# The assumed delay of an instruction page in an issue-order planner: SLOW from 7000 to 8900, FAST from 3500 to 3900

## The chip, the cores and the metric

One core of a Trainium2 chip runs the whole program. The metric is the time of one execution in device microseconds, as the median of several runs. Five engines work side by side and meet at semaphores: TensorE (PE for its matmuls, PEld for its weight loads), VectorE (DVE), ScalarE (ACT), GpSimd (POOL) and SyncE (SP), which here only issues DMAs.

## What is computed

A decaying linear attention over 2 batches, 8 heads, 768 positions and 64 values a head, in blocks with a running state, and behind it two small networks on the 1536 tokens of 512 values, all in fp32:

```python
intra = einsum(einsum(q_b, k_b) * Dmask, v_b);  inter = einsum(q_b * lam_pow, kv_state)
out_b = intra + inter                                 # attention, block by block
kv_state = lam_block * kv_state + einsum(k_b * rev_pow, v_b)
x = (sigmoid(x @ w_gate) * (x @ w_val)) @ w_out       # 512 -> 1536 -> 512
h = x @ w_in2;  y = where(h > 0, h, exp(min(h, 0)) - 1) @ w_out2   # 512 -> 2048 -> 512
```

## The kernel before

**Work.** The attention goes through six chunks of 128 positions (`for c in range(NCH)`). For a chunk, `scores` multiplies keys and queries (tile `st`) and, from the second chunk on, the decayed keys `kd` with the values of the chunk before (written to the same banks, so also `st` in a profile); VectorE applies the decay (`pr`), TensorE multiplies by the values and by the state (tile `x`; the state is `sn`), and `split_chunk` makes the operands of the first network from the result. These attention products are plain fp32: each takes two passes, and so four instructions (two weight loads, two matmuls), on few columns. A block of 16 or 32 of them is issued in one piece (`together`).

The networks run on fp32r operands split into a high and a low part, three products for one, with a seven-product scheme for 2x2 blocks (`product`) and with `unit` for the output matrices. The first group of gate and value weights is multiplied without that scheme for the first two chunks (`direct`): 24 matmuls of 256 columns for each of gate and value and each chunk, two instructions each. In the profile they carry the tile names `direct` and `warm`, since the bank A0 was first named by the 18 warm-up matmuls that open the kernel.

**Order.** Nothing runs as it is recorded. The program's engine calls only record operations (`Work.record`, hence one line, L182, stands for nearly all instructions in the profile). `Work.issue` then works out dependences (`hazards`), lays out a time plan many times (`run`, L310: ten settings of two parameters, seven forward passes each, keys from a backward pass in between), lets `exchange` combine the best stretches of different plans, and emits all five engines' instructions in the order of the plan with the earliest end. The order is then fixed in the program; the times of the plan are not.

**Pages in the plan.** TensorE's instructions lie in pages of 256 (`PAGE`), the first one already holding 63 others (`FIRST`). `run` counts the words (instructions) it has put on TensorE in `told`. In `stall` (inside `run`) there are two marks for page m: at word 256m - 63 - 293 (`LEAD`) the fetch of page m is taken to begin, and the page is usable `SLOW` ns later when the planned DMA queue still has over 2 us to go, otherwise `FAST` ns later; at word 256m - 63 TensorE needs the page, and the plan adds what is missing. When the operation that is due would stall by over 100 ns, another ready operation within `thrift` (20 us of rank) that stalls for nothing is put ahead of it, the one with the fewest words first:

```python
if mark == m * self.PAGE - self.FIRST:
    late += max(0.0, here.get(m, pages.get(m, 0)) - now)
else:
    here[m] = now + (self.SLOW if queue > now + 2000 else self.FAST)
...
if e == "tensor" and not backward and thrift and stall(ops[k], t) > 100:
    like = min((x for x in ripe[e] if x[0] < rank + thrift and not stall(ops[x[1]], t)), default=None,
               key=lambda x: (ops[x[1]].words, x))
```

Of the kernel before, what the change touches and what calls it, by code (L numbers as in the profile page):

```python
# [127 lines left out]
class Work:  # L128
    MATMUL = {512: (229, 391), 384: (173, 335), 256: (120, 283)}
    SWITCH, TABLE = 150, 1283  # L130
    PAGE, LEAD, FIRST, SLOW, FAST = 256, 293, 63, 7000, 3500
    HANDOFF = {"tensor": 60, "vector": 35, "scalar": 35, "gpsimd": 78, "sync": 30}
    OVERLAP = {"vector": 83, "scalar": 101, "gpsimd": 45}

# [953 lines left out]
```

## Time and profile before

| | us |
|---|---|
| median of 3 runs (lowest, highest) | 584.72 (584.50, 584.95) |
| the profiled execution's own time | 584.14 |
| its span, first to last instruction | 582.4 |
| PE busy in the span | 572.2 |
| PEld busy | 492.2 |
| DVE, ACT, POOL busy | 388.9, 304.3, 312.3 |

The granted TensorE clock has a mean of 0.999 of full speed. Some 1.7 us of the profiled execution lie outside its span. The names in a row are out<-in, with the shape of one instruction and xN for how many; in brackets stands the engine's idle time ahead of the group and what ended it. "issue" is time in which the engine waited for nothing that the profile can name.

### The profile page before, as it was taken

To read this page: it belongs to the slowest core of one execution; us is meant where nothing else is said; L and a number is where in the kernel's file an instruction comes from. 1 tells how busy PE (TensorE), PEld (TensorE's weight loads), DVE (VectorE), ACT (ScalarE), POOL (GpSimd) and SP (SyncE) were. 2 spreads that over 40 slices of the span, in tenths; PEclk is the share of its full clock that TensorE was granted. 3 is DMA by queue.
4 is the path that set the end of the run, shared out by engine and by line. 5 is a ranking of instruction groups with operands and counts; after the bars stand their busy time and mean duration, and the time that the engine had idled before them with its cause. 6 is when DMAs were issued, how large, how long until landed. Compare 5 with 4: busy or idle time off the path is not lost.

```text
span 582.4 us, 10132 instructions
## 1 busy us (share of the span) xinstructions
PE 572.2 (98%) x4021; PEld 492.2 (85%) x4022; DVE 388.9 (67%) x687; ACT 304.3 (52%) x588; POOL 312.3 (54%) x265
## 2 busy tenths in 40 slices
PE   7899999999999999999999999999999999999997
PEld 4788898888888888888999888888888888888886
DVE  7785842586466467367549994888778666867474
ACT  4993656551442443344138987774556464645250
POOL 2677778587376276476237964574817272552100
PEclk9999999999999999999999999999999999999999
DMA  8936211422122122222100112242222211100004
GB/s 301 411 160 218 74 74 74 145 73 85 60 73 89 56 72 73 73 74 74 72 2 6 69 72 74 73 144 73 73 73 73 73 74 72 35 38 1 1 37 180
DMA packets 10271, 52.03 MB, mean 89 GB/s; under 512 B 1264, under 2 KB 1520, under 8 KB 5744
## 3 DMA queue, kind: packets, MB, share of 16 engines
q1 hardware_dynamic: 10224, 51.39, 24.3%
q8 instruction: 31, 0.51, 0.4%
q14 instruction: 16, 0.13, 0.1%
HBM read 48.24 MB, written 3.15 MB: 88 GB/s over the span
## 4 chain that ended last, share of the span: by engine, by line
PE 87%; ACT 4%; DVE 4%; DMA 3%; issue 1%; SPq 0%; ACTq 0%; DVEq 0%
PE xu L182 34%; PE st L182 31%; PE direct L182 10%; PE warm L182 9%; PE x L182 2%; DMA w<-in_w_val 1%; ACT sig L182 1%; DMA w<-in_w_gate 1%; DVE w L182 1%; DVE sums L182 1%; ACT w L182 1%; DVE xu L182 1%; DVE sig L182 0%; ACT L182 0%; ACT x143h L182 0%
## 5 line engine op out<-in xcount | busy, mean ns | idle before, releaser
L182 PE MATMUL xu<-gl,woh 128*128 128x512 f32 (+1 forms) x306 | 119.9, 392 | 0.0
L182 PE MATMUL xu<-gh,woh 128*128 128x512 f32 (+1 forms) x306 | 119.1, 395 | 0.2 <-DVE acc L182 0.2
L182 PE MATMUL xu<-gh,wol 128*128 128x512 f32 (+1 forms) x306 | 118.9, 389 | 0.0
L182 DVE TENSOR_TENSOR acc<-xu,acc 128x512 f32<-128x512 f32 x120 | 80.6, 686 | 42.2 <-PE xu L182 40.1
L182 POOL TENSOR_TENSOR gl<-sig,gh 128x1024 fp32r<-128x1024 f32 (+1 forms) x38 | 74.3, 1969 | 49.7 <-ACT gh L182 41.5
L182 POOL TENSOR_TENSOR t<-w 128x256 f32<-128x256 f32 (+1 forms) x80 | 68.8, 887 | 48.2 <-DVE w L182 46.1
L182 POOL TENSOR_TENSOR l<-t,h 128x768 fp32r<-128x768 f32 (+1 forms) x38 | 60.0, 1588 | 42.2 <-ACT h L182 22.2
L182 PEld LDWEIGHTS xu<-gh,woh 128*128 128x128 f32 x306 | 57.2, 188 | 12.8 <-DVE acc L182 1.5
L182 PEld LDWEIGHTS xu<-gh,wol 128*128 128x128 f32 x306 | 57.5, 188 | 11.7
L182 PEld LDWEIGHTS xu<-gl,woh 128*128 128x128 f32 x306 | 57.6, 188 | 10.5 <-POOL gl L182 0.9
L182 POOL TENSOR_TENSOR wol<-w,woh 128x512 fp32r<-128x512 f32 x26 | 33.3, 1299 | 54.7 <-ACT woh L182 54.7
L182 ACT CAST gh<-sig 128x512 fp32r<-128x512 f32 (+1 forms) x58 | 45.3, 785 | 23.8 <-DVE sig L182 22.7
L182 DVE SCALAR_TENSOR_TENSOR w<-w,w 128x1024 uint32<-128x1024 uint32 (+1 forms) x36 | 55.4, 1542 | 0.5
L182 ACT ACTIVATE w<-w 128x1024 f32<-128x1024 f32 (+1 forms) x36 | 39.0, 1084 | 27.7 <-POOL wol L182 12.6
L182 DVE TENSOR_TENSOR wt<-st,wt 128x512 f32<-128x512 f32 (+1 forms) x57 | 32.0, 561 | 31.7 <-PE st L182 30.5
L182 PE MATMUL st<-x143l,h 128*128 128x512 f32 (+1 forms) x150 | 51.6, 347 | 0.0
L182 PE MATMUL st<-x143h,h 128*128 128x512 f32 (+1 forms) x150 | 51.4, 347 | 0.0
L182 PE MATMUL st<-x143h,l 128*128 128x512 f32 (+1 forms) x150 | 51.1, 346 | 0.0
L182 ACT ACTIVATE sig<-st 128x512 f32<-128x512 f32 (+1 forms) x52 | 29.3, 565 | 27.9 <-PE st L182 18.7
L182 DVE TENSOR_SCALAR w<-w 128x1024 uint32<-128x1024 uint32 (+1 forms) x36 | 27.7, 772 | 24.0 <-ACT w L182 23.4
L182 ACT ACTIVATE sig<-warm 128x256 f32<-128x256 f32 (+1 forms) x35 | 13.7, 391 | 48.9 <-PE warm L182 24.5
L182 ACT CAST h<-t 128x768 fp32r<-128x768 f32 (+1 forms) x40 | 29.1, 728 | 11.7 <-POOL t L182 8.0
(179 smaller groups left out, 1402.5 us busy)
## 6 DMA issues: line engine op xcount, KB each, us to landing
w<-in_w_out SPq DMA_DIRECT2D x14, 1024.0 KB, 4.7
w<-in_w_in SPq DMA_DIRECT2D x8, 1024.0 KB, 4.8
nat<-in_att SPq DMA_DIRECT2D x12, 512.0 KB, 9.7
w<-in_w_gate SPq DMA_DIRECT2D x5, 1024.0 KB, 4.8
w<-in_w_val SPq DMA_DIRECT2D x5, 1024.0 KB, 4.8
tin<-in_att SPq DMA_DIRECT2D x6, 512.0 KB, 8.8
tin<-in_att SPq DMA_DIRECT2D x3, 1024.0 KB, 11.4
out_t<-o SPq DMA_DIRECT2D x11, 256.0 KB, 2.0
```

The source lines that it names most:

```text
L182: return [getattr(getattr(self.nc, eng), fn)(*(real(a) for a in args), **{k: real(a) for k, a in kw.items()})]
```

## The change

Two numbers of the planner's class change. No operation, tile or DMA of the kernel is added or removed; what can change is the order in which `issue` emits them, on all engines.

```diff
 class Work:
     MATMUL = {512: (229, 391), 384: (173, 335), 256: (120, 283)}
     SWITCH, TABLE = 150, 1283
-    PAGE, LEAD, FIRST, SLOW, FAST = 256, 293, 63, 7000, 3500
+    PAGE, LEAD, FIRST, SLOW, FAST = 256, 293, 63, 8900, 3900
```

## Rows read from the trace of the kernel before

**Rows 1.** Stretches: us, busy (x instructions) by engine, clock, DMA share, GB/s.
```profile
24.00:30.50 6.50, 6.26 (x143) 5.83 (x144) 5.26 (x10) 6.50 (x24) 3.97 (x5) 1.00 1.03 413
37.00:43.00 6.00, 6.00 (x127) 5.63 (x129) 5.53 (x15) 4.92 (x15) 4.19 (x4) 1.00 0.02 5
43.00:582.40 539.40, 535.73 (x3302) 462.37 (x3294) 355.47 (x608) 271.42 (x499) 289.10 (x240) 1.00 0.21 73
```

**Rows 2.** Waits of PE from 0 to 43 us: total, times, longest.
```profile
PE st L182 <- issue: 2.1, 2, 1.1
PE st L182 <- ACT sn L182: 0.7, 1, 0.7
```

**Rows 3.** Waits of PE from 43 us to the end.
```profile
PE xu L182 <- DVE acc L182: 0.2, 1, 0.2
```

**Rows 4.** PE in order of time: start, us, group, idle before it.
```profile
15.95 0.33 PE L182 MATMUL st<-nat,kd 128*64 128x64 f32 x3
17.39 0.62 PE L182 MATMUL st<-nat,kd 128*64 128x64 f32 x13 [1.11 <-issue]
...
35.55 0.45 PE L182 MATMUL st<-nat,kd 128*64 128x64 f32 x6
36.96 0.51 PE L182 MATMUL st<-nat,kd 128*64 128x64 f32 x10 [0.96 <-issue]
...
39.83 0.51 PE L182 MATMUL direct<-x11h,h 128*128 128x256 f32 x2
40.17 0.40 PE L182 MATMUL direct<-x11h,x143l 128*128 128x256 f32 x2
```

**Rows 5.** The page's DMA queues: packets, MB, share.
```profile
q8 instruction: 31, 0.51, 0.4%
```

**Rows 6.** Instructions since the start, columns as in Rows 1 (PE, then PEld).
```profile
0.00:8.45 8.45, 6.53 (x77) 3.27 (x79) 5.19 (x22) 3.48 (x9) 0.89 (x7) 1.00 0.71 235
0.00:15.09 15.09, 11.70 (x203) 7.39 (x208) 10.93 (x31) 7.16 (x17) 4.67 (x11) 1.00 0.85 306
...
0.00:17.38 17.38, 12.89 (x222) 8.24 (x223) 11.87 (x33) 9.45 (x25) 6.96 (x13) 1.00 0.87 320
0.00:23.91 23.91, 18.61 (x333) 13.04 (x335) 18.00 (x44) 15.00 (x36) 10.50 (x15) 1.00 0.91 344
0.00:28.20 28.20, 22.90 (x462) 17.00 (x463) 21.21 (x48) 19.29 (x50) 13.07 (x17) 1.00 0.93 355
0.00:30.49 30.49, 24.96 (x476) 18.97 (x478) 23.34 (x53) 21.58 (x58) 14.55 (x19) 1.00 0.94 359
...
0.00:36.95 36.95, 30.46 (x603) 24.13 (x605) 27.85 (x65) 27.97 (x75) 18.98 (x23) 1.00 0.89 343
...
0.00:42.67 42.67, 36.17 (x717) 29.46 (x718) 33.05 (x79) 32.76 (x89) 22.90 (x26) 1.00 0.77 298
0.00:46.75 46.75, 40.25 (x862) 33.27 (x867) 36.10 (x86) 34.31 (x92) 26.98 (x28) 1.00 0.74 284
```

**Rows 7.** The chain that ended last, up to 60 us: start, us, what.
```profile
10.17 8.63 DMA w<-in_w_val
...
30.26 0.24 issue
...
31.50 2.16 PE warm L182 x18
...
36.00 0.96 issue
```

**Rows 8.** ACT in order of time.
```profile
23.60 0.60 ACT L182 COPY sn<-st 128x128 f32<-128x128 f32 x3
...
32.07 0.61 ACT L182 ACTIVATE sig<-direct 128x512 f32<-128x512 f32 x1
```

**Rows 9.** A later stretch, columns as in Rows 1, and its costliest DVE group there.
```profile
306.00:337.50 31.50, 31.30 (x203) 28.22 (x201) 29.83 (x74) 27.26 (x66) 24.58 (x22) 1.00 0.10 34
...
L182 DVE TENSOR_TENSOR xu<-xu,acc 128x512 f32<-128x512 f32 x11 | 7.6, 694 | 1.3 <-PE xu L182 1.2
```

## The prediction

> **What bounds the kernel now.** First the stretches. From 43 us to the end PE is busy 535.73 of 539.40 us [rows 1], and the waits of PE in that part come to two of 0.2 us, one of which is shown [rows 3]. TensorE's work there is the same whatever the order, so its length can hardly fall; it can only grow. What an order can win lies ahead of 43 us. There the waits say "issue" twice for 2.1 us [rows 2] and the chain of waits shows a third of 0.24 us [rows 7]: PE stood still and the profile names nothing that it waited for.
>
> Then the counts, to see what these three are. Up to the first of them, at 17.38 us, 222 matmuls and 223 weight loads had started: 445 instructions; up to 30.49 us 954, up to 36.95 us 1208 [rows 6]. The steps are 509 and 254, two pages and one page of 256, less a few instructions that are no matmul or load. The planner's marks 256m - 63 for m = 2, 4, 5 are 449, 961, 1217. So each of the three stands at a page's first word, two of them in the middle of a block that was issued in one piece [rows 4]. The page's queue table has 31 instruction packets [rows 5], one for each later page: three of 31 crossings cost 1.11 + 0.24 + 0.96 = 2.31 us, the others none that is listed.
>
> Last, how late a page is. For page 2 the fetch mark (word 156) is reached at 8.45 us, and the stalled word starts at 17.39: 8.94 us. For page 5, word 924 at 28.20 and the word at 36.96: 8.76 us. For page 4, word 668 at 23.91 and the chain's wait ends at 30.50: 6.59 us [rows 4, 6, 7]. The old plan allowed 7.0 in all three. The new 8.9 fits pages 2 and 5 and is 2.3 us too long for page 4. DMA shares of 1.03 at 24 to 30.5 us and 0.02 at 37 to 43 us [rows 1] say that these are the pages fetched while loads are queued.
>
> **The change, part by part.** Operations and DMAs stay as they are; only orders move.
>
> Page 5. In the old plan it was due at 28.20 + 7.0 = 35.2 us, so a block of `kd` products that began at 35.55 looked free [rows 4]. With 8.9 it is due at 37.1, the planner sees over a microsecond of stall and puts two-word matmuls ahead. Are there any? The 24 value products of chunk 1 run from 39.83 on [rows 4]; their bank was free when ScalarE had read it at 32.07 + 0.61 = 32.68 us [rows 8], so those that use the high parts were ready. How many fit is set by words, not by time: six matmuls and their loads, 12 words, had gone through before the stall [rows 4], so six direct matmuls fit ahead of the mark. One takes 2.16 / 18 = 0.12 us [rows 7], six 0.72. Going from fp32 to fp32r costs 0.51 - 0.40 = 0.11 us for the first pair [rows 4], taken twice for there and back: 0.22. This wait lies on the chain, so the gain is 0.72 - 0.22 = 0.50 us. Bounds: nothing, and 0.96 - 0.22 = 0.74 where a whole block changes places with more such matmuls.
>
> Page 4. On the chain too, 0.24 us; it stood inside a run of direct matmuls, so no extra change of type is needed. Gain 0.24; at least 0.
>
> Page 2. Due at 8.45 + 8.9 = 17.35 instead of 15.45. Its 1.11 us are not on the chain: there the chain runs through the load of the value weights (10.17 to 18.80) and ScalarE's work behind it [rows 7]; PE then waits 0.7 us for `sn` [rows 2], whose copies end at 23.60 + 0.60 = 24.2 [rows 8]. If PE is 1.11 us earlier, it waits 1.8 us for `sn`. I take 0. Bounds: 0, and 1.11 if ScalarE's order moves as well, so that `sn` comes ahead of the value weights' conversion.
>
> Page 3. Fetch mark (411 instructions) at 15.09, due at 23.99; PE is held by `sn` at word 668 until 23.91 and has 37 more words to go [rows 2, 6]. It gains nothing.
>
> Later pages, with 3.9 for 3.5. The tightest is page 7: 1435 instructions at 42.67, 1729 at 46.75, 4.08 us apart [rows 6], still over 3.9. Behind it 256 words take 256 x 539.40 / 6596 = 21 us on the mean [rows 1]. Zero.
>
> The wrong 2.3 us of page 4. The planner now believes in a stall until 23.91 + 8.9 = 32.8 us and may pull up to 2.3 / 0.12 = 19 direct matmuls ahead of attention blocks. That work is used up when the attention's own waits come, from 37 to 49 us. Cost 0 to 2.3 us; I take 0, since PE has no listed wait from 37 to 43 us [rows 1].
>
> All other stretches. The planner starts from another set of plans, so the order behind 43 us may change too. Gain at most the two waits of 0.2 us; loss at least 0 and bounded by no row. I take 0.
>
> Sum: 0.50 + 0.24 = 0.74 us off. The profiled execution took 584.14 us, 582.4 of it the span, and would take 583.4. The median of the runs is 0.58 us above it, so I forecast 584.72 - 0.74 = **584.0 us**. Something like 0.2%, or 1.17 us, is what a measurement of this kernel can tell from no change; the forecast lies inside it.
>
> **A rule that speaks against the change.** Three crossings of 31 cost 2.31 us in all [rows 2, 5, 7]. The Trainium skill (Runtime: NRT & Kernel Launch, section "Instruction fetch mechanics") says that an engine gets its instructions in blocks of 16 KiB, 256 instructions, and that the cost of crossing is "mostly hidden". By that rule alone the sum would be 0 and the time 584.7. The trace agrees for 28 crossings and not for these three.
>
> **The rivals.**
>
> *All three waits go.* Page 2 counts if `sn` moves ahead. For it: the new due times hit pages 2 and 5 within 0.2 us. Against it: the chain at 10 to 19 us is a DMA [rows 7]. 2.31 less two changes of type of 0.22 is 1.87: 582.8 us.
>
> *The wait is only handed on.* PE reaches its next producer sooner and waits there as long, as with `sn`; or the best plan stays the same, and the program with it. Against it: two of the waits are on the chain. 584.7 us. It is what the skill's rule above would give as well.
>
> *Slower: page 4 is believed 2.3 us too late.* Place: PE between 30 and 49 us. The direct matmuls go ahead of score and state blocks, VectorE and ScalarE get these later, and PE has nothing left to fill in with. Price: up to 2.3, less 0.74: 1.6 us, 586.3 us. It decides as soon as new waits there exceed 0.74 us. For it: 6.59 measured against 8.9 believed. Against it: that the plan also counts the delay of the attention.
>
> *Slower: a later passage loses its fit.* From 306 to 337.5 us PE is busy 31.30 of 31.50 us with DVE at 29.83 and ACT at 27.26 [rows 9]: nobody has room. An order in which three more of DVE's 0.694 us operations [rows 9] stand ahead of what PE needs costs 2.1 us, less 0.74: 586.1 us. It decides with the second such operation. For it: any new plan may do this. Against it: the old plan, made by the same costs, lost only 0.4 us behind 43 us [rows 3].
>
> **How the numbers follow.** The forecast has 0.40; its own range is 583.2 to 584.5 (a gain of 1.5 to 0.2 us), of which 0.10 lies beyond 0.2%. All three waits: 0.22, all of it faster. Handed on: 0.14, the same. Page 4: 0.14, slower. A later passage: 0.10, slower. Faster 0.10 + 0.22 = 0.32, the same 0.30 + 0.14 = 0.44, slower 0.14 + 0.10 = 0.24. The range goes from 582.2, where all three waits go without a change of type (584.72 - 2.31 = 582.4) and a 0.2 us wait with them, to 586.5, just over the two slower cases.
>
> **What would show it.** The waits of PE up to 43 us: "issue" down from 2.3 us to about 1.6 or less, with direct matmuls where the `kd` blocks met pages 2 and 5. If page 2's wait is gone and that for `sn` is about 1.8 us, the step on the chain was right. Behind 43 us the waits should stay below 0.5 us. I am wrong if "issue" stays above 2 us, if new waits for DVE or ACT between 30 and 49 us exceed 0.7 us, or if a wait over 0.5 us appears behind 43 us.

## The result, and the profile after

The changed kernel takes 587.90 us (median of 5 runs, 586.69 to 589.27) against 584.72 before (584.11 to 585.37): a ratio of 1.0056, 95% interval 1.0039 to 1.0074, so 3.3 us slower. The profiled execution took 587.77 us, its span is 586.0 against 582.4. PE is busy for 573.3 us, about as long as before (572.2); what was added is time in which it stands still, or runs at half clock. All five executions have a mean granted clock of 0.996 or 0.997; one stretch of 3.4 us at half clock takes a mean over 586 us down to 0.997. One execution of a later kernel, lead256, took 596.52 us, far above the others of its kernel, and is left out of its figures.

The waits of PE over the whole span of the changed kernel (total, times, longest; answers to [rows 2, 3]):

```profile
PE x L182 <- DVE sums L182: 1.6, 1, 1.6
...
PE warm L182 <- issue: 1.0, 1, 1.0
PE x L182 <- issue: 0.9, 1, 0.9
PE direct L182 <- issue: 0.8, 1, 0.8
...
PE st L182 <- issue: 0.5, 1, 0.5
...
PE x L182 <- DVE x22l L182: 0.3, 1, 0.3
```

Two things stand here. The "issue" waits are four instead of three and come to 3.2 us, where the forecast said 1.6 or less. And two waits for VectorE are new, 1.6 and 0.3 us.

PE in order of time shows where the four are (start, us, group, idle before it; compare [rows 4]):

```profile
17.76 0.38 PE L182 MATMUL warm<-x11l,x143h 128*128 128x256 f32 x1 [1.04 <-issue]
...
24.23 1.11 PE L182 MATMUL st<-tin 64*64 64x128 f32 x40 [0.49 <-issue]
...
30.70 0.51 PE L182 MATMUL direct<-x11l,h 128*128 128x256 f32 x2 [0.82 <-issue]
...
37.07 0.45 PE L182 MATMUL x<-pr,nat 128*64 128x64 f32 x6 [0.88 <-issue]
```

These are the first words of pages 2 to 5. In the kernel before, pages 2, 4 and 5 came at 17.39, 30.50 and 36.96 [rows 4, 7]: another order, and within 0.4 us the same times. From one to the next it is 6.47, 6.47 and 6.37 us here, and 6.46 from page 4 to page 5 before. The counts of the changed kernel say how far that is from the planner's rule (instructions since the start, PE and then PEld in brackets; the marks 293 words ahead of pages 2 to 5):

```profile
0.00:8.83 8.83, 6.83 (x77) 3.18 (x78) 4.47 (x19) 3.29 (x8) 0.88 (x7) 1.00 0.73 241
0.00:15.84 15.84, 12.63 (x204) 7.82 (x207) 11.15 (x34) 8.12 (x20) 3.17 (x10) 1.00 0.86 315
0.00:23.02 23.02, 18.62 (x334) 12.80 (x334) 15.90 (x45) 13.81 (x38) 6.78 (x13) 1.00 0.91 344
0.00:27.80 27.80, 22.91 (x462) 16.61 (x462) 17.69 (x50) 18.57 (x49) 7.24 (x14) 1.00 0.93 356
```

From mark to page it is 8.93, 8.39, 7.68 and 9.27 us: no constant. In these two kernels a page follows 6.4 to 6.5 us behind the first word of the page before it, and in both page 5 begins at 37 us.

Most of the loss is at 59 to 79 us (PE busy 18.06 of 20 us), where the profile before has nothing (19.89 of 20 us from 58 to 78). PE of the changed kernel in stretches (us, busy (x matmuls), granted clock, DMA share, GB/s), then PE and VectorE in order of time:

```profile
64.00:66.00 2.00, 0.39 (x6) 1.00 0.26 53
66.00:68.00 2.00, 1.67 (x52) 0.83 1.00 422
68.00:70.00 2.00, 2.00 (x41) 0.50 0.15 57
70.00:72.00 2.00, 2.00 (x26) 0.82 0.00 0
```

```profile
65.83 0.33 PE L182 MATMUL x<-pr,nat 64*64 64x64 f32 x4 [1.61 <-DVE sums L182]
66.49 2.44 PE L182 MATMUL x<-pr,nat 64*64 64x64 f32 x60 [0.33 <-DVE x22l L182]
68.86 1.99 PE L182 MATMUL x<-ql,sn 64*64 64x128 f32 x32
```

```profile
60.93 0.68 DVE L182 TENSOR_SCALAR w<-w 128x1024 uint32<-128x1024 uint32 x1
...
62.53 1.58 DVE L182 SCALAR_TENSOR_TENSOR w<-w,w 128x1024 uint32<-128x1024 uint32 x1
64.04 0.41 DVE L182 TENSOR_TENSOR xt<-x,xa 128x256 f32<-128x256 f32 x1
...
64.70 1.07 DVE L182 TENSOR_TENSOR sums<-x,xa 128x256 f32<-128x256 f32 x3
...
66.03 0.41 DVE L182 TENSOR_TENSOR x22l<-x,x22h 128x256 fp32r<-128x256 f32 x1
```

Chunk 5's `x` needs the banks that the split of chunk 4 (`xt` to `x22l`) still reads, and VectorE has put the conversion of the first output weights (`w`, 0.68 and 1.58 us) ahead of that split. PE stands for 1.9 us; behind that the granted clock is 0.5, its 1.2 GHz level, for some 3.4 us (all of 68 to 70, and 0.7 us on either side).

### The profile page after: what moved, and what is told of

It reads as the page before. It is cut to its first block, busy times and chain, and to the rows that moved or that the text cites. A ratio compares the mean times of both kernels' runs of the same rounds, so it can differ in the third digit from the quotient of the medians.

```text
span 586.0 us, 10113 instructions
## 1 busy us (share of the span) xinstructions
PE 573.3 (98%) x4022; PEld 492.2 (84%) x4022; DVE 374.1 (64%) x687; ACT 302.6 (52%) x588; POOL 310.0 (53%) x265
## 4 chain that ended last, share of the span: by engine, by line
PE 91%; DMA 3%; DVE 3%; issue 1%; ACT 1%; SPq 0%; DVEq 0%; ACTq 0%
PE xu L182 37%; PE st L182 32%; PE direct L182 10%; PE warm L182 9%; PE x L182 2%; DMA w<-in_w_gate 2%; DMA w<-in_w_val 1%; ACT w L182 1%; DVE sums L182 1%; DVE pr L182 1%; DVE xu L182 0%; DVE w L182 0%; SPq L182 0%; DVE sig L182 0%; DVE xt L182 0%
## 5 line engine op out<-in xcount | busy, mean ns | idle before, releaser
L182 DVE SCALAR_TENSOR_TENSOR w<-w,w 128x1024 uint32<-128x1024 uint32 (+1 forms) x36 | 46.9, 1305 | 0.3
L182 DVE TENSOR_SCALAR w<-w 128x1024 uint32<-128x1024 uint32 (+1 forms) x36 | 26.5, 737 | 32.2 <-ACT w L182 32.1
L182 ACT ACTIVATE sig<-sig 128x256 f32<-128x256 f32 (+1 forms) x68 | 34.5, 508 | 1.4
```

Source lines behind the costliest of these rows:

```text
L182: return [getattr(getattr(self.nc, eng), fn)(*(real(a) for a in args), **{k: real(a) for k, a in kw.items()})]
```

## The experiments

Theory A: the loss is VectorE's order at 59 to 66 us, with the half clock behind it. Theory B: it is the pages and the order ahead of 43 us. Theory C, formed behind the first four runs: what costs is that a new order is drawn at all. The planner's class is the same in all kernels; edits that move operations name them by their number in the recording. Ratios are to the kernel before, run beside the others on the same chip: its median was 585.03 us beside the first four experiments, 584.68 beside the other constants and 584.62 beside the rest.

**VectorE's conversion behind the split.**

```diff
         order = sorted(range(n), key=lambda k: (best[1][k], k))
+        moved = [670, 671, 675]      # the two conversions, and the load that follows them
+        order = [k for k in order if k not in moved]
+        at = order.index(453) + 1
+        order[at:at] = moved
...
```

> The changed kernel with one thing moved: VectorE's two conversions of the first output weights (0.68 and 1.58 us), which stand ahead of the split of chunk 4, come behind it. Theory A (VectorE's order at 59 to 66 us is the loss): ScalarE's copies end near 63.0 us, the split's operations of 0.33 us then end near 65.0 instead of 66.4, so PE's wait of 1.6 + 0.3 us for them falls to about 1.0, and if the half clock of 67.3 to 70.7 us comes from that wait, the blocks behind it take 2.9 us again instead of 4.4. Together 1 to 2.5 us less: 585.4 to 586.9. Theory B (the instruction pages and the order ahead of 43 us are the loss): 587.9, within 0.5 us.

Measured 587.19 us, ratio 1.0034 (1.0021 to 1.0047), where the change itself had 1.0056. Waits of PE behind 43 us:

```profile
PE x L182 <- DVE sums L182: 1.0, 1, 1.0
...
PE st L182 <- POOL wol L182: 0.5, 2, 0.3
...
PE direct L182 <- DVE wt L182: 0.3, 1, 0.3
PE x L182 <- DVE x22l L182: 0.3, 1, 0.3
```

The wait shrank as worked out, 1.6 to 1.0, and the mean clock is 1.0 again in all four executions. But the time is 0.3 us above the expected 585.4 to 586.9: `wol`, made from the converted weights, is now late at 72 to 74 us, and `wt` at 80. VectorE has no gap from 70.0 to 73.8 us; part of the wait is handed on. The gain over the change, 0.0022 or 1.3 us with an uncertainty as large, is no more than the clock alone gives in the next experiment, so what the shorter wait is worth is not shown.

And 1.3 of the 1.9 us of wait are still there with the conversions out of the way. PE's own order left the split less room, as rows show that no run tries by itself. The last block of chunk 4 and the first of chunk 5, in the kernel before and then the last block of chunk 4 in the changed one:

```profile
57.35 1.10 PE L182 MATMUL x<-ql,sn 64*64 64x128 f32 x32
...
63.00 1.13 PE L182 MATMUL x<-pr,nat 64*64 64x64 f32 x32
```

```profile
61.50 1.10 PE L182 MATMUL x<-ql,sn 64*64 64x128 f32 x32
```

Before, 5.65 us lie between their starts; in the changed kernel PE was ready for chunk 5's `x` at about 64.1 us, 2.6 us behind 61.50. VectorE's conversions are thus a part of the wait, and not the larger one.

**The wait filled.** 14 matmuls without use ahead of operation 537, chunk 5's first `x`:

```diff
+                if k == 537:
+                    for x in self.fillers:
+                        x.call()
...
+            for k in range(14):
+                nc.tensor.matmul(banks[0][:, 0:256], lhsT=wV["M2"][0][:, 0], rhs=xops[0]["22", "h"][:, 0],
+                                 start=True, stop=True, skip_group_check=True)
...
```

> The changed kernel with 14 more matmuls of 256 columns (0.12 us each, 1.7 us) in PE's wait at 64.06 to 65.83 us; their product is used by nobody. They do no useful work, so the wait stays as long. If the half clock that follows comes from PE standing still, the granted clock stays at full speed from 67 to 71 us and the blocks there take 2.9 us instead of 4.4: 1.5 us less, 586.4. If it comes from the fp32 blocks themselves, the clock falls as before and the time is 587.9 or slightly above.

Measured 587.16 us, 1.0034 (1.0021 to 1.0048). PE in order of time, and then the stretch from 68 us:

```profile
64.05 1.84 PE L183 MATMUL st<-x11h,h 128*128 128x256 f32 x14
65.81 0.33 PE L183 MATMUL x<-pr,nat 64*64 64x64 f32 x4
66.47 1.76 PE L183 MATMUL x<-pr,nat 64*64 64x64 f32 x60 [0.33 <-DVE x22l L183]
68.17 1.10 PE L183 MATMUL x<-ql,sn 64*64 64x128 f32 x32
```

```profile
68.00:70.00 2.00, 2.00 (x47) 1.00 0.22 86
```

`x` comes at the same time as in the changed kernel (65.81 against 65.83), but the clock stays at 2.4 GHz and the two groups take 1.76 + 1.10 us instead of 2.44 + 1.99: 1.57 us less. All four executions have a mean clock of 0.999 or 1.0, where all five of the change have 0.996 or 0.997. So it is the standing still that the half clock followed. Of the 1.57 us the ratio shows 1.3 (0.0022 x 584.72), though the two intervals overlap; the trace has a wait of 1.1 us for VectorE's `sig` further on that the changed kernel has with 0.2.

**The reverse, in the kernel before.**

```diff
+        moved = [671]                # the conversion that stood behind the split
+        order = [k for k in order if k not in moved]
+        at = order.index(670) + 1
+        order[at:at] = moved
...
```

> The kernel before with the reverse: VectorE's conversion of 1.83 us at 64.06 us comes ahead of the split of chunk 4 at 59.97. Theory A: the split and the scores of chunk 5 end 1.8 us later, PE has its next chunk-5 block waiting at 63.0 and waits some 1.8 us; with a fall of the clock behind it 1.5 us more: 586.5 to 588.1. Theory B (pages): no page is met there, 584.7.

Measured 586.79 us, 1.0024 (1.0012 to 1.0036), inside A's range and above B's 584.7. In the trace, a wait and a clock as in the changed kernel (waits; then stretches of PE as above):

```profile
PE warm L182 <- ACT sig L182: 2.0, 1, 2.0
```

```profile
64.00:66.00 2.00, 2.00 (x24) 0.57 0.96 406
66.00:68.00 2.00, 2.00 (x36) 0.58 0.00 0
```

The wait is for ScalarE's `sig`, which waits for VectorE: one operation moved on VectorE is enough for both parts of the loss in this trace. What A had not said is that another reader of VectorE's work would be late first. The median mixes two kinds of execution: six of the ten, the profiled one among them, have a mean clock of 0.994 to 0.997 and took 586.67 to 587.64 us (mean 587.16), the other four 1.0 and 584.97 to 585.91 (mean 585.53). In one and the same program the half clock thus cost 1.6 us, and without it only 0.5 us over the kernel before (585.03) is left; how long PE waits in those four no trace shows.

**The step of the prediction by itself: ready work into the wait at page 5.**

```diff
+        moved = list(range(253, 271))     # 18 direct matmuls of chunk 1's values
+        order = [k for k in order if k not in moved]
+        at = order.index(312)
+        order[at:at] = moved
...
```

> The kernel before with 18 ready direct matmuls of chunk 1's values (2.16 us, 36 words) moved from 39.8 us to ahead of the fp32 block that starts at 34.54, so that page 5's first word comes up later than 36.96 us. The prediction's own step (the wait at a page is idle time that ready work fills): the wait of 0.96 us goes, one change of type of 0.22 is added, 0.7 us less: 584.0. A rival (PE only reaches its next producer sooner): 584.7. A second rival (a page comes a fixed time behind the mark 293 words ahead, and the mark moves too): the wait stays in part, with page 5's first word behind 37.0 us.

Measured 585.51 us, 1.0008 (0.9999 to 1.0017): no gain. PE's waits, and where the new one lies:

```profile
PE x L182 <- DVE sums L182: 0.9, 1, 0.9
PE st L182 <- issue: 0.7, 1, 0.7
...
PE direct L182 <- issue: 0.3, 1, 0.3
```

```profile
43.93 0.33 PE L182 MATMUL x<-pr,nat 64*64 64x64 f32 x4 [0.89 <-DVE sums L182]
44.59 1.59 PE L182 MATMUL x<-pr,nat 64*64 64x64 f32 x54 [0.33 <-DVE x22l L182]
```

Page 5's wait is gone; 1.2 us of waiting for the split of chunk 2 has come at 43.9. The first rival of the expectation holds. The last operation of that split, in the kernel before and then here:

```profile
43.09 0.41 DVE L182 TENSOR_TENSOR x22l<-x,x22h 128x256 fp32r<-128x256 f32 x1
```

```profile
44.12 0.42 DVE L182 TENSOR_TENSOR x22l<-x,x22h 128x256 fp32r<-128x256 f32 x1
```

PE came to the `x` block at 43.04 us, 1.06 us earlier than before (44.10). But the moved matmuls take longer than the wait that they fill, so the fp32 blocks behind them were put off (chunk 2's `x<-ql,sn` begins at 39.82 instead of 38.80), and the split ends 1.04 us later. A fill no longer than the wait, the six matmuls of the forecast, was not run.

**Other constants.** Four more orders, each drawn by the planner from other numbers; in this order they are slow7100, slow8800, lead256 and lead256_fast2500:

```diff
-    PAGE, LEAD, FIRST, SLOW, FAST = 256, 293, 63, 7000, 3500
+    PAGE, LEAD, FIRST, SLOW, FAST = 256, 293, 63, 7100, 3500
+    PAGE, LEAD, FIRST, SLOW, FAST = 256, 293, 63, 8800, 3900
+    PAGE, LEAD, FIRST, SLOW, FAST = 256, 256, 63, 6450, 3500
+    PAGE, LEAD, FIRST, SLOW, FAST = 256, 256, 63, 6450, 2500
```

> The kernel before with SLOW at 7100 instead of 7000, FAST left at 3500: 0.1 us on a page is nothing that the pages could feel, but the planner draws a new order. Theory C (what costs is the new order as such, since the old one fits unusually well from 55 to 75 us): slower than before by some 2 to 3.5 us, 586.5 to 588.5, with new waits of PE for VectorE or ScalarE behind 43 us. Theory B (the longer assumed delay is what costs): 584.7 within 0.6 us.

> SLOW at 8800 with FAST at 3900, next to the change. Theory C: again another order, 586 to 588.5, with its waits at other places than the changed kernel's 64 us. If the value itself decided, the same waits at 64 us and a half clock behind them, 587.9.

> The planner with the page rule that both traces show: the fetch begins at the first word of the page before (LEAD 256 for 293) and the page is usable 6450 ns later while loads are queued (FAST 3500). If a truer page rule helps, the issue waits of PE fall from 2.3 us to about 1 and the time is below 584.7, 583 to 584.5. Theory C: the pages ahead of 43 us don't decide, the new order costs behind 43 us: 586 to 588.5, whatever the issue waits do.

> As the run with LEAD 256 and SLOW 6450, with FAST 2500. Another draw: by theory C 586 to 588.5 and different waits behind 43 us; by the theory that a truer page rule helps 583 to 584.5.

| kernel | PE's issue waits, us | us | ratio (95%) |
|---|---|---|---|
| before | 2.5 | 584.72 | 1 |
| the change | 3.2 | 587.90 | 1.0056 (1.0039 to 1.0074) |
| before, page 5 filled | 1.0 | 585.51 | 1.0008 (0.9999 to 1.0017) |
| slow7100 | 1.7 | 586.11 | 1.0025 (1.0015 to 1.0035) |
| slow8800 | 0.5 | 589.48 | 1.0087 (1.0068 to 1.0106) |
| lead256 | 1.2 | 589.18 | 1.0065 (1.0039 to 1.0091) |
| lead256_fast2500 | 1.5 | 586.27 | 1.0024 (1.0011 to 1.0036) |

The waits are those of the one profiled execution; 0.16 us of the 2.5, and of those of the last four, lies at 8 us and at no page. All six are slower than before or the same, and the issue waits don't go with the time: the order that waits least for pages is the slowest. Its waits ahead of 43 us, and the stretch behind the longest:

```profile
PE st L182 <- ACT sn L182: 2.5, 1, 2.5
...
PE warm L182 <- issue: 0.5, 2, 0.3
```

```profile
24.00:28.00 4.00, 4.00 (x97) 0.58 1.02 416
```

What it saves at the pages it waits for `sn`, and the half clock is behind that wait again. In lead256_fast2500 too the clock decides much: six executions with a mean of 0.996 or 0.997 took 586.73 us on the mean, the four with 0.999 or 1.0 took 585.11. Not so in slow7100, where nine of ten kept 0.999 or 1.0. That 0.1 us on SLOW makes the kernel 1.4 us slower (slow7100) says that the draw itself is a large part. Theory C had the sign of all four and was loose in size: 586.11 lies just below its range, 586.27 inside, 589.48 and 589.18 above. The waits of slow8800 are not those of the change, though SLOW is nearly the same. The truer page rule of the last two brought the issue waits down and not the time, so that theory fell. FAST alone at 3900 gives the program of before, instruction for instruction, and SLOW alone at 8900 that of the change.

**Cutting the two orders together.** The planner runs with both pairs of constants; the first part of the issue order is one's, the rest stands as the other has it. The limit is a time of the plan: 53.5 us there is some 57 us in the trace, 72 is 76 and 44 is 46. The edit of the first cut:

```diff
+        for self.SLOW, self.FAST, until in ((8900, 3900, 53500), (7000, 3500, 1e9)):
...
+            orders.append([k for k in order if best[1][k] < until])
+        order = orders[0] + sorted(set(orders[1]) - set(orders[0]), key=orders[1].index)
```

> Both plans are made; the first 57 us of the issue order are the changed kernel's, everything behind stands in the order of the kernel before. Up to there the two traces have lost the same (for the same matmul work the clock differs by under 0.2 us), although PE's issue waits differ, 3.2 us against 2.5. Theory A (the loss is the passage at 59 to 78 us): as before, 584.7 within 0.7. Theory B (the pages and the order ahead of 43 us are the loss): 587 to 588.

> The reverse cut: the first 57 us in the order of the kernel before, everything behind in the changed kernel's. Theory A: PE's wait for the split of chunk 4 near 64 us is there, with or without the half clock behind it: 586.5 to 588. Theory B: 584.7 within 0.7.

> The first 76 us in the order of the kernel before, the rest in the changed kernel's. Theory A: no wait near 64 us, and only the 0.5 us that the changed kernel's trace loses behind 78 us: 585.2 within 0.7. A rival (the later passages near 306 to 337 and 390 us are the loss): 587 or more.

| first part, rest | us | ratio (95%) |
|---|---|---|
| change to 57 us, then before | 585.27 | 1.0013 (1.0003 to 1.0022) |
| before to 57 us, then change | 587.97 | 1.0057 (1.0043 to 1.0070) |
| before to 76 us, then change | 585.30 | 1.0012 (1.0002 to 1.0021) |

The second is as slow as the whole change, and its trace has the same wait and the same fall of the clock (waits; then stretches of PE). One of its four executions kept a mean clock of 0.999 and took 586.79 us, the others 587.85 to 588.50.

```profile
PE x L182 <- DVE sums L182: 1.6, 1, 1.6
```

```profile
64.00:68.00 4.00, 2.10 (x46) 0.86 0.61 219
68.00:72.00 4.00, 4.00 (x70) 0.72 0.12 47
```

Between the second and the third lies the passage from 57 to 76 us alone: 0.0057 - 0.0012 = 0.0045, or 2.6 of the 3.3 us. What is behind 76 us costs 0.7 us (0.1 to 1.2). The first 57 us of the change cost nothing that shows when followed by its own rest; followed by the other rest they cost 0.8 us, part of it a wait of 1.1 us for ScalarE's `sig` at 61.9 us, behind the seam, that neither kernel has.

**A try at a faster kernel:** slow7100's first 46 us, then before's order.

> The first 46 us in the order that SLOW 7100 gives, whose trace had done the same matmul work there some 2 us earlier than the kernel before, the rest in the order of the kernel before. If what is gained ahead of 46 us stays: 582.7 to 583.5, faster than both kernels. If it is handed on to the split and state operations of the next chunks: 584.7.

Measured 585.44 us, 1.0014 (1.0005 to 1.0023): handed on, and more. Behind 43 us PE waits 0.8 us for VectorE's `sig` and 0.7 for ScalarE's `x11h`, and the clock has fallen again in

```profile
50.00:60.00 10.00, 9.63 (x137) 0.83 0.47 179
```

The fall is not what the time hangs on here: the seven executions with a mean clock of 0.996 or 0.997 took 585.48 us on the mean, the four others 585.26.

No version found here is faster than the kernel before.

## Why the prediction was wrong

- **What bounds the kernel** held. Behind 43 us a new order could only lose, and the three waits were pages. Two of the forecast's own signs of being wrong came: "issue" waits of 3.2 us (over 2), and one of 1.6 us behind 43 us (over 0.5).
- **The delay of a page** was read as mark plus 8.9 us because two of three fitted. The changed kernel's own pages are 7.68 to 9.27 us behind their marks and 6.4 to 6.5 us behind each other. The change brought no page forward, it only changed which work lies ahead of one. The 6.59 us of page 4 hang on the count besides: five instructions ahead of its mark are no matmul or load, and with them the mark is passed at 22.77 us, ahead of PE's wait for `sn`, instead of 23.91. By that count page 4 was 7.7 us late, and the new 8.9 is 1.2 us too long for it, not 2.3.
- **Page 5, 0.50 us, with page 4's 0.24: failed.** The step said that a wait on the chain that is filled with ready work is a gain, and that the planner would fill it. The planner did not: the waits at the pages rose from 2.3 to 3.2 us, page 4's from 0.24 to 0.82, and the order put another fp32 block across page 5 (0.88 us). Filled by hand in the kernel before, with 18 matmuls, the wait went and nothing was gained (1.0008): what PE had won, 1.06 us, it gave back in a wait of 1.2 us for VectorE's split. Whether six would have paid stays open; the split ended 0.6 us ahead of the `x` block (43.50 against 44.10), so there was room for 0.6 us at most.
- **Page 2 at 0** was not put to the test by the change, which still waits there (1.04 us). slow8800 bears the reason out: 0.34 us of wait at page 2, and 2.5 us for `sn` behind it. Page 3, taken as free, has a wait of 0.49 us.
- **FAST at 0** was exactly right: it changes no instruction.
- **"All other stretches. I take 0"** is the step that decided, and it failed: 3.3 us net, 2.6 of it between 57 and 76 us. I wrote that the loss there is bounded by no row, and then took the end of the range that no row supported either. The only argument was that the old plan, made with the same costs, lost 0.4 us. One good draw did not tell the next; the five draws here all lost 1.4 us or more.
- **The rivals.** The last had the mechanism, VectorE operations ahead of what PE needs, at 306 to 337 us and for 2.1 us, with 0.10. It was at 59 to 66 us: 1.9 us of wait, of which VectorE's conversions account for 0.6, and, which no rival had, 1.57 us of half clock behind it. Page 4's rival expected its loss at 30 to 49 us; nothing is lost there.
- **The page's rule.** The Trainium skill (Runtime: NRT & Kernel Launch, "Instruction fetch mechanics") calls the cost of crossing a block of instructions "mostly hidden". The trace of the changed kernel agrees for 27 of 31 crossings and not for four, which wait 3.2 us. Over the orders tried here, with 0.5 to 3.2 us of such waits, the time does not follow them.

## What to carry to other kernels

When a parameter feeds a search that redraws the whole order, the first cost to price is the redraw: in five draws of five here the order that fitted unusually well was lost, whatever the parameter was to repair. Try a change that should mean nothing (0.1 us here) to see how far a redraw alone moves the time, and cut two orders together at a time mark to find the stretch that pays. A stall on the chain is worth at most the slack to the next producer behind it: before counting the stall as a gain, read when that one is ready, and whether the filling itself makes it later.

## What was unexpected in the hardware

After PE had stood still for 1.9 us at 64 us the granted clock fell from 2.4 to 1.2 GHz and came back some 3.4 us later; with 14 useless matmuls in the wait it stayed up, which is worth 1.57 us in the trace. The kernel before waits 1.11 us at 16 us without a fall, and the last kernel fell behind waits of 0.7 and 0.8 us, so the length of one wait does not settle it. Nor does the program alone: by their mean clocks, the reverse in the kernel before fell in six executions of ten, and the kernel before itself in four of 23 on that chip (mean 585.60 us against 584.83) and in none of 46 on two others. What does settle it stays open. And with loads queued (DMA share 1.03 from 17.4 to 30.5 us, 0.63 from there to 37) an instruction page comes every 6.4 to 6.5 us in the two kernels, and from page 4 to page 5 in the other traces that wait at both 6.2 (slow7100) to 7.0 us (before to 76 us, then change). That it is the queued loads that make it so slow was not tried by itself.
